# One pair of states transposed by a DMA instead of TensorE, and the operations up to batch 4's first product in another order

## The chip, the core and the metric

The kernel runs on one core of a Trainium2 chip. A core has TensorE (PE, matrix products into PSUM), VectorE (DVE), ScalarE (ACT), GpSimd (POOL) and SyncE (SP); each runs its own queue of instructions in order, and semaphores tie the queues together. The metric is the device time of one launch in microseconds, as the median of several runs.

## The reference

There are 8 batches, 8 heads, 512 tokens, 32 states and 64 numbers per head. Tokens read from the states and states read from the tokens by softmax attention; both results of a batch, 512 + 32 rows of 512 numbers, go through a layer of three products of which the largest counts, and an output product.

```python
scores = scale * np.matmul(x, state.transpose(0, 1, 3, 2))
a = softmax(scores);   xread = np.matmul(a, state)
a2 = softmax(scale * np.matmul(state, x.transpose(0, 1, 3, 2)));   sread = np.matmul(a2, x)
...
x = concatenate([xread, sread]) as [4352, 512]
h = np.maximum(np.maximum(x @ w1, x @ w2), x @ w3)     # 512 -> 768
return (h @ w_out).astype(np.float32)                  # 768 -> 512
```

## The kernel before

The products are reassociated: a token's reading of the states followed by w1, w2, w3 is the attention weights times G = states x weights, so each batch has its own G.

The work is cut into small operations, and their order is written out by hand in the string `PLAN`. One function per operation issues its instructions; each engine takes its own instructions in the order of the plan. `BANKS` and `PAIRS` say which of the four single PSUM banks and two double ones each result takes, in the order of the plan; `PLACES` gives the slot of each SBUF buffer. A result can be written into a bank only when the copies out of the bank's last use are done.

The names that matter here (b is a batch, k a pair of batches, so states 3 serve batches 6 and 7):

- `stc k`, `stt k`, `stp k`: cast the states, transpose them on TensorE (four transposes into a bank), and copy them in two halves into the block layout `bd`. `std k` does the transposing as a DMA from SyncE's queue into an SBUF buffer `stT`; it is defined in the kernel before, and not used by its plan.
- `lx b`, `lxg b g`: load x, whole or half, from GpSimd's queue. `xtd b`: transpose x by DMA, SyncE's queue. `pad b`: copy x with a column of ones, on GpSimd.
- `sc b`, `ex b`, `sum b`: scores (PE), exponentials (ACT), sums and their reciprocals (DVE). `wt b`: the weights, multiplied on GpSimd. `atd b`: the weights transposed by DMA on SyncE's queue into `aT`.
- `sr b`, `srs b`, `srt b`: the states' own reading (PE), scaled (DVE), transposed by DMA (SyncE).
- `g`, `gr b c0 c1`, `gq b c0 c1`: a slice or a run of columns of G on TensorE; `gr` takes a double bank, `gq` two single ones. `gc`, `grc`, `gqc` copy it out, on the engines that the last letters name.
- `l1 b m`: three chains of two products into three banks. `m0` copies the first on ScalarE, `ma` and `mb` take the maximum with the second and third on VectorE, into `ht`.
- `l2 b j`: six products with the output weights; `l2c` copies the result out; `so` stores, from the queue of its last letter.
- `ones` first waits, on GpSimd, for the output weights to land.

SyncE's queue holds the transposing DMAs in the plan's order, GpSimd's the loads, the pads, the weights and most stores. The lines to follow in the profile: 261 (`stt`), 265 (`std`), 271 (`stp`), 291 (`xtd`), 349 (`wt`), 366 (`atd`), 375 (`pad`), 201 and 206 (`lx`, `lxg`), 427 (`g`, `gr`, `gq`), 466 and 469 (`grc`, `gqc`), 477 (`l1`), 492 (`m0`), 497 (`ma`), 505 (`mb`), 514 (`l2`), 526 (`l2c`), 548 (`so`).

Of the kernel before, what the change touches and what calls it, by code (L numbers as in the profile page):

```python
# [15 lines left out]


PLAN = """
    lst 0 A; lxu 0 0 S; zero; clr 0; clr 1; clr 2; clr 3; warm; lxg 0 1; busy 1; xones 1; ident; busy 1;
    lxg 1 0; busy 1; busy 1; stc 0 D; busy 1; busy 1; busy 1; busy 1; busy 1; lxg 1 1; stt 0; busy 1; busy 1;  # L20
    cxu 0 0 D; xt 0 0; stp 0 A; busy 1; xt 0 1; lw 0 2 1; lw 0 1 0; xtc 0 0 D; sc 0 0; xones 0; lw 0 2 2;
    xtc 0 1 D; busy 1; busy 1; sc 0 1; xt 1 0; ex 0 0; ex 0 1; lw 1 3 0; sum 0 0; sum 0 1; xtc 1 0 A; busy 1;
    busy 1; xt 1 1; sc 1 0; xtc 1 1 D; ex 1 0; busy 1; busy 1; sc 1 1; lw 2 3 2; wt 0 1 D; lw 2 3 1; lw 3 4 0;
    wt 0 0 P; lw 3 6 2; at 0 0; sr 0; ex 1 1; sr 1; g 0 0; sum 1 0; wt 1 0 P; g 1 0; atc 0 0 A; at 0 1; at 1 0;
    gc 0 0 A; atc 0 1 A; g 1 1; sum 1 1; gc 1 0 D; atc 1 0 A; srs 0; srs 1; g 0 1; wt 1 1 P; at 1 1; gc 0 1 A;
    l1 0 0; atc 1 1 D; lst 1 A; m0 0 0; lst 3 A; gc 1 1 A; ma 0 0; lw 3 6 1; lw 4 6 0; lxg 2 1; lxg 2 0; l1 0 1;
    m0 0 1; lwo; mb 0 0; g 0 2; g 1 2; ma 0 1; l1 1 0; lst 2 A; gc 0 2 A; mb 0 1; m0 1 0; ma 1 0; l1 0 2;
    mb 1 0; gc 1 2 A; m0 0 2; ma 0 2; l1 1 1; m0 1 1; g 1 3; stc 1 P; mb 0 2; ma 1 1; g 0 3; mb 1 1; stt 1;
# [15 lines left out]
    ma 3 1; l1 3 2; m0 3 2; mb 3 1; ma 3 2; l1 3 3; m0 3 3; mb 3 2; ma 3 3; l1 3 5; wt 4 - P; m0 3 5; mb 3 3;
    l2 2 2; grc 4 1280 1792 A; grc 4 512 1024 A; ma 3 5; mb 3 5; l2c 2 2 D; l1 3 4; so 2 2 4 P; m0 3 4; ma 3 4;
    lx 6; mb 3 4; atd 4; srt 1; ap 0 A; so 2 0 2 P; pad 5; gr 5 1792 2304; gr 5 0 512; grc 5 1792 2304 AD;
    l2 3 0; l2 3 1; grc 5 0 512 D; l2c 3 0 A; l1 4 0; m0 4 0; sc 5 -; ex 5 -; xtd 6; l2c 3 1 D; l2 3 3; ma 4 0;
    gq 5 1024 1280; gr 5 1280 1792; gr 5 512 1024; mb 4 0; sr 5; gqc 5 1024 1280 A; sum 5 -; srs 5; l2c 3 3 A;
    l1 4 1; m0 4 1; ma 4 1; l1 4 2; m0 4 2; mb 4 1; ma 4 2; l1 4 3; m0 4 3; mb 4 2; ma 4 3; l1 4 5; wt 5 - P;
    m0 4 5; mb 4 3; l2 3 2; grc 5 1280 1792 A; grc 5 512 1024 A; ma 4 5; mb 4 5; l2c 3 2 D; l1 4 4; so 3 2 4 P;  # L50
    m0 4 4; ma 4 4; lx 7; mb 4 4; atd 5; srt 2; ap 1 A; so 3 0 2 P; pad 6; gr 6 1792 2304; gr 6 0 512;
    grc 6 1792 2304 AD; l2 4 0; l2 4 1; grc 6 0 512 D; l2c 4 0 A; l1 5 0; m0 5 0; sc 6 -; ex 6 -; xtd 7;
    l2c 4 1 D; l2 4 3; ma 5 0; gq 6 1024 1280; gr 6 1280 1792; gr 6 512 1024; mb 5 0; sr 6; gqc 6 1024 1280 A;
    sum 6 -; srs 6; l2c 4 3 A; l1 5 1; m0 5 1; ma 5 1; l1 5 2; m0 5 2; mb 5 1; ma 5 2; l1 5 3; m0 5 3; mb 5 2;
    ma 5 3; l1 5 5; wt 6 - P; m0 5 5; mb 5 3; l2 4 2; grc 6 1280 1792 A; grc 6 512 1024 A; ma 5 5; mb 5 5;
    l2c 4 2 D; l1 5 4; so 4 2 4 P; m0 5 4; ma 5 4; mb 5 4; atd 6; srt 3; ap 2 A; so 4 0 2 P; pad 7;
    gr 7 1792 2304; gr 7 0 512; grc 7 1792 2304 AD; l2 5 0; l2 5 1; grc 7 0 512 D; l2c 5 0 A; l1 6 0; m0 6 0;
    sc 7 -; ex 7 -; l2c 5 1 D; l2 5 3; ma 6 0; gq 7 1024 1280; gr 7 1280 1792; gr 7 512 1024; mb 6 0; sr 7;
    gqc 7 1024 1280 A; sum 7 -; srs 7; l2c 5 3 A; l1 6 1; m0 6 1; ma 6 1; l1 6 2; m0 6 2; mb 6 1; ma 6 2;
    l1 6 3; m0 6 3; mb 6 2; srt 4; ma 6 3; l1 6 5; wt 7 - P; m0 6 5; mb 6 3; l2 5 2; grc 7 1280 1792 A;  # L60
    grc 7 512 1024 A; ma 6 5; mb 6 5; l2c 5 2 D; l1 6 4; so 5 2 4 P; m0 6 4; ma 6 4; mb 6 4; atd 7; ap 3 A;
    ap 4 A; so 5 0 2 P; srt 6; l1 7 0; srt 7; m0 7 0; l2 6 0; ap 7 D; srt 5; ma 7 0; mb 7 0; l1 7 2; m0 7 2;
    ap 6 A; l2c 6 0 D; ma 7 2; l1 7 3; m0 7 3; ap 5 A; mb 7 2; ma 7 3; l1 7 4; m0 7 4; l2 6 1; l2c 6 1 A;
    ma 7 4; mb 7 4; l1s 0; m0 s 0; l2 6 2; l2c 6 2 A; look; ma s 0; mb s 0; so 6 2 3 S; mb 7 3; l1 7 1; m0 7 1;
    ma 7 1; l1s 2; m0 s 2; mb 7 1; ma s 2; l1 7 5; m0 7 5; mb s 2; ma 7 5; l1s 1; m0 s 1; ma s 1; so 6 0 1 S;
    mb 7 5; l1s 5; m0 s 5; l2p 7 2 384 512; ma s 5; mb s 1; mb s 5; l1s 3; m0 s 3; l2pc 7 2 384 512 A;
    l2p 7 0 384 512; l2p 7 3 256 512; sop 7 2 384 512 P; ma s 3; l2p 7 2 128 384; mb s 3; l2p 7 0 0 128;
    l2pc 7 0 0 128 A; l2pc 7 3 256 512 D; l2p 7 1 0 128; l2pc 7 0 384 512 D; l2p 7 3 0 256; flag;
    l2pc 7 1 0 128 A; l2pc 7 2 128 384 A; l1s 4; m0 s 4; l2 6 3; sop 7 0 0 128 P; ma s 4; sop 7 0 384 512 P;
    mb s 4; l2p s 0 256 512; so 6 1 2 P; l2 s 1; sop 7 3 256 512 A; l2c 6 3 D; l2p 7 2 0 128; sop 7 1 0 128 S;  # L70
    so 6 3 4 A; l2pc 7 3 0 256 D; l2p s 0 0 256; l2pc s 0 256 512 D; sop s 0 256 512 A; l2pc 7 2 0 128 A;
    l2p 7 1 128 384; sop 7 2 0 128 A; l2p 7 0 256 384; l2pc s 0 0 256 A; l2pc 7 1 128 384 A; l2c s 1 D;
    l2p 7 1 384 512; l2p 7 0 128 256; sop 7 3 0 256 S; sop 7 2 128 384 P; l2pc 7 0 256 384 D; sop 7 1 128 384 A;
# [12 lines left out]
PLACES = """
    xT 0:0 1:1 2:2 3:0 4:1 5:2 6:0 7:1;
    e 0:0 1:1 2:0 3:1 4:0 5:1 6:0 7:1;
    a 0:0 1:1 2:0 3:1 4:0 5:1 6:0 7:1;
    aT 0:0 1:1 2:2 3:0 4:1 5:2 6:0 7:1;  # L90
    G 0:0 1:1 2:2 3:0 4:1 5:2 6:0 7:1;
    ht 0:0 1:1 2:2 3:3 4:0 5:1 6:2 7:3;
    osb x00:0 0:1 1:2 2:0 3:1 4:2 5:0 6:1 7:2 s:0;
    xp 2:0 3:1 4:0 5:1 6:0 7:1;
    t0 00:0 01:1 10:2 02:0 11:1 12:2 03:0 13:1 05:2 14:0 04:1 15:2 20:0 21:1 22:2 23:0 25:1 24:2 30:0 31:1 32:2 33:0
        35:1 34:2 40:0 41:1 42:2 43:0 45:1 44:2 50:0 51:1 52:2 53:0 55:1 54:2 60:0 61:1 62:2 63:0 65:1 64:2 70:0
        72:1 73:2 74:0 s0:1 71:2 s2:0 75:1 s1:2 s5:0 s3:1 s4:2;
    t1 00:0 01:1 10:2 02:0 11:1 12:2 03:0 13:1 05:2 14:0 04:1 15:2 20:0 21:1 22:2 23:0 25:1 24:2 30:0 31:1 32:2 33:0
        35:1 34:2 40:0 41:1 42:2 43:0 45:1 44:2 50:0 51:1 52:2 53:0 55:1 54:2 60:0 61:1 62:2 63:0 65:1 64:2 70:0
        72:1 73:2 74:0 s0:1 71:2 s2:0 75:1 s1:2 s5:0 s3:1 s4:2;  # L100
    st 0:0 1:1 2:0 3:1
"""


# [639 lines left out]
```

## Time and profile before

| what | value |
|---|---|
| median of 3 runs | 152.14 us (152.1 to 152.29) |
| span of the profiled execution | 150.5 us; no other time is recorded for it |
| TensorE | 145.1 us busy, 96% of the span |
| VectorE | 118.0 us, 78% |
| ScalarE | 83.2 us, 55% |
| GpSimd | 56.1 us, 37% |

The span reaches from the first to the last instruction, and the runs' time takes in what lies around it. A row of the chain gives start, length, engine, output tile and line; a row of the timeline or of a group gives the output and input tiles, their shapes, the count of instructions, and in brackets the idle time before them with what ended it. Durations of products are those of one instruction, which overlaps with the next; the cost of a product in a full stream is read from the distance of two starts.

### The profile page before, as it was taken

What the parts mean: (1) busy time and instruction counts of PE and PEld (TensorE: products, weight loads), DVE (VectorE), ACT (ScalarE), POOL (GpSimd) and SP (SyncE); (2) the same over time, 40 slices, a digit from 0 to 9 for tenths busy, and PEclk for the clock granted to TensorE, in tenths of its full rate; (3) what the DMA queues carried; (4) which work ended last, traced back from release to release, by engine and by line L of the source; (5) the groups of instructions that cost most, each with busy time, mean ns of one, the idle gap of its engine ahead of it and who ended that gap; (6) DMA issues with size and microseconds to landing.
All of it is one profiled execution on the core that took longest, in us unless ns stands there. A gap on an engine that the chain in (4) does not pass through costs nothing.

```text
span 150.5 us, 3618 instructions
## 1 busy us (share of the span) xinstructions
PE 145.1 (96%) x1422; PEld 72.8 (48%) x1422; DVE 118.0 (78%) x202; ACT 83.2 (55%) x144; POOL 56.1 (37%) x78
## 2 busy tenths in 40 slices
...
GB/s 121 195 188 189 206 230 198 196 97 139 124 97 171 235 182 189 108 209 178 145 102 216 183 139 90 231 183 131 157 4 78 121 175 7 139 0 17 190 199 167
DMA packets 39108, 22.29 MB, mean 148 GB/s; under 512 B 23072, under 2 KB 36896, under 8 KB 39088
## 3 DMA queue, kind: packets, MB, share of 16 engines
...
q8 instruction: 12, 0.20, 0.6%
...
## 4 chain that ended last, share of the span: by engine, by line
PE 88%; DMA 5%; POOL 3%; issue 1%; DVE 1%; ACT 1%; POOLq 0%
PE pw L477 47%; PE po L514 25%; PE pg L427 6%; DMA w<-in_moe_w_dram 5%; PE po L532 4%; PE ps L305 2%; PE psr L391 2%; POOL w L217 1%; POOL x L206 1%; PE pgh L427 1%; ACT G L444 1%; PE pt L261 1%; DVE held L593 0%; PE idle L591 0%; PE pat L358 0%
## 5 line engine op out<-in xcount | busy, mean ns | idle before, releaser
L477 PE MATMUL pw<-aT,G 128*128 128x512 bf16 x288 | 66.7, 379 | 0.0
L492 ACT CAST t<-pw 128x512 bf16<-128x512 f32 (+1 forms) x54 | 30.5, 564 | 27.3 <-PE pw L477 26.4
L497 DVE TENSOR_TENSOR t<-t,pw 128x512 bf16<-128x512 bf16 (+1 forms) x54 | 35.3, 654 | 11.1 <-ACT t L492 8.9
L477 PEld LDWEIGHTS <-G 128*128 128x128 bf16 x288 | 27.1, 98 | 32.8 <-issue 2.1
L514 PE MATMUL po<-wout,ht 128*128 128x512 bf16 x168 | 39.7, 379 | 0.0
L505 DVE TENSOR_TENSOR ht<-t,pw 128x512 bf16<-128x512 bf16 x48 | 32.9, 686 | 4.5
L349 POOL TENSOR_TENSOR a<-e,rden 128x1024 bf16<-128x1024 bf16 (+1 forms) x9 | 14.6, 1622 | 27.2 <-ACT osb L526 11.1
L514 PEld LDWEIGHTS <-ht 128*128 128x128 bf16 x168 | 15.4, 98 | 19.0 <-issue 1.7
L548 POOL DMA_DIRECT2D out_dram<-osb x13 | 7.4, 571 | 27.5 <-ACT t L492 27.5
L466 ACT CAST G<-pg 128x1024 bf16<-128x1024 f32 (+1 forms) x17 | 14.7, 895 | 2.1 <-PE pg L427 2.1
L526 ACT COPY osb<-po 128x512 f32<-128x512 f32 x15 | 8.9, 592 | 9.1 <-PE po L514 9.1
L526 DVE COPY osb<-po 128x512 f32<-128x512 f32 x14 | 9.6, 688 | 3.9 <-PE po L514 3.8
L375 POOL COPY xp<-x 128x1024 bf16<-128x1024 bf16 x12 | 12.3, 1059 | 0.0
L313 ACT ACTIVATE e<-ps 128x1024 bf16<-128x1024 f32 (+1 forms) x10 | 8.5, 854 | 6.7 <-PE ps L305 6.7
L466 DVE CAST G<-pg 128x1024 bf16<-128x1024 f32 (+1 forms) x12 | 11.6, 995 | 0.0
L342 DVE TENSOR_REDUCE seen<-e 128x32 f32<-128x1024 bf16 (+1 forms) x10 | 10.0, 997 | 1.7 <-ACT e L313 1.7
L427 PE MATMUL pg<-w,bd 64*32 64x512 bf16 (+1 forms) x288 | 10.7, 362 | 0.4 <-DMA w<-in_moe_w_dram 0.2
L444 ACT CAST G<-pg 128x768 bf16<-128x768 f32 x10 | 8.0, 810 | 2.7 <-PE pg L427 2.5
...
L249 PE MATMUL idle<-zero 128*128 128x512 bf16 x18 | 7.4, 506 | 1.8 <-DVE zero L225 1.3
L477 PE MATMUL pw<-atp,w 128*128 128x256 bf16 x72 | 8.7, 272 | 0.0
...
## 6 DMA issues: line engine op xcount, KB each, us to landing
out_dram<-osb POOLq DMA_DIRECT2D x12, 512.0 KB, 3.7
x<-in_x_dram POOLq DMA_DIRECT2D x4, 512.0 KB, 7.2
...
```

The lines of the kernel that those rows point to most:

```text
L342: nc.vector.reduce_sum(out=den, in_=parity(e[b], g), axis=AX.X)
L349: times[c](out=parity(a[b], g).rearrange("p j g s n -> p j (g s) n"), in0=parity(e[b], g).rearrange("p j g s n -> p j (g s) n"), in1=rdens ...
L375: nc.gpsimd.tensor_copy(out=xp[b][:, :, :, g * (D + 1):g * (D + 1) + D], in_=v[:, g])
L427: nc.tensor.matmul(p(s, g), bd(b, 2 * s + g)[64 * g:64 * g + 64, g, :], f(w_sb[64 * g:64 * g + 64, s]), start=True, stop=True, tile_positi ...
L444: copier[c[g]](out=G[b][:, g:h, :, m * 128:m * 128 + 128], in_=p[:, g:h, 0:384].rearrange("p g (i f) -> p g i f", i=3))
L466: copier[c[g]](out=v[:, g:h], in_=p[:, g:h, 0:c1 - c0])
L477: nc.tensor.matmul(pw[i][:, 0:n], lhs(i, k), rhs(k), start=(k == 0), stop=(k == nk - 1))
L492: nc.scalar.copy(out=t0s[b, m][:, 0:n], in_=open_ps["l", b, m][0][:, 0:n])
L497: nc.vector.tensor_max(t1s[b, m][:, 0:n], t0s.pop((b, m))[:, 0:n], open_ps["l", b, m][1][:, 0:n])
L505: nc.vector.tensor_max(ht[b][:, m, :], t1s.pop((b, m))[:, 0:n], open_ps.pop(("l", b, m))[2][:, 0:n])
L514: nc.tensor.matmul(p, ht[b][:, m, tokens(b, j)], wout_sb[:, m, :], start=(m == 0), stop=(m == NM - 1))
L526: copier[c[i]](out=o[:, j, i * w:i * w + w], in_=p[:, i * w:i * w + w])
```

## The change

`stt 3` (four transposes on TensorE) becomes `std 3` (one transposing DMA on SyncE's queue, behind `xtd 5` and ahead of `atd 4`), and its copies, `stp 3`, go from ScalarE, ahead of `l2c 0 2`, to GpSimd, behind `pad 5`. Three copies change engines: `l2c 1 0` from VectorE to ScalarE, the first half of `grc 3 0 512` from ScalarE to VectorE, `l2c 2 0` from ScalarE to VectorE. On GpSimd, `pad 2` comes ahead of `ones` and of the loads of batch 3, `lx 4` ahead of the first two stores, which trade places, and `pad 4` ahead of `lx 5`. On SyncE, `srt 0` comes directly behind `atd 2`. On TensorE, `gr 3 1280 1792` comes ahead of `gq 3`. On VectorE, `mb 1 4` comes ahead of its half of `stp 2` and of `stc 3`; on ScalarE, `l2c 2 3` comes ahead of `gqc 4`. Some other operations stand elsewhere in the plan with their place in each queue unchanged. `BANKS` loses the bank of `stt 3` and is renumbered in places, `PAIRS` changes in the third group, and `PLACES` gets `stT 2:0 3:0`. Everything ahead of `gr 2 0 512` and everything from `gr 5 1792 2304` on is in the same order as before.

Cut to the reordered lines, without the two ends that only wrap differently:

```diff
-    ma 1 3; l1 0 5; stc 2 P; g 1 5; gr 2 0 512; mb 1 3; m0 0 5; ma 0 5; l1 1 4; gc 1 5 A; gr 2 1280 1792;
-    m0 1 4; grc 2 0 512 D; mb 0 5; gr 2 512 1024; ma 1 4; grc 2 1280 1792 AD; l1 0 4; m0 0 4; ma 0 4; stt 2;
-    mb 0 4; sc 2 -; ex 2 -; grc 2 512 1024 D; stp 2 AD; stc 3 D; mb 1 4; l2 0 3; l2 0 0; l2c 0 3 A; l2c 0 0 A;
-    sum 2 -; l2 0 1; ones; pad 2; lxg 3 0; lxg 3 1; wt 2 - P; stt 3; xtd 3; l2c 0 1 A; l1 1 5; pad 3;
-    so 0 0 2 P; lx 4; m0 1 5; l2 0 2; ma 1 5; mb 1 5; stp 3 A; l2c 0 2 A; l2 1 0; gq 2 1024 1280; gr 3 0 512;
-    gr 3 1792 2304; l2c 1 0 D; grc 3 1792 2304 D; gqc 2 1024 1280 A; grc 3 0 512 A; atd 2; sr 2; l2 1 1; srs 2;
-    sc 3 -; l1 2 0; m0 2 0; ex 3 -; l2c 1 1 D; l2 1 3; ma 2 0; gq 3 1024 1280; so 0 2 4 P; gqc 3 1024 1280 A;
-    l2c 1 3 A; gr 3 512 1024; gr 3 1280 1792; mb 2 0; sum 3 -; wt 3 - P; atd 3; xtd 4; srt 0; sr 3; srs 3;
...
-    ma 2 4; lx 5; mb 2 4; so 1 0 2 P; pad 4; gr 4 1792 2304; gr 4 0 512; grc 4 1792 2304 AD; l2 2 0; l2 2 1;
-    grc 4 0 512 D; l2c 2 0 A; l1 3 0; m0 3 0; sc 4 -; ex 4 -; xtd 5; l2c 2 1 D; l2 2 3; ma 3 0; gq 4 1024 1280;
-    gr 4 1280 1792; gr 4 512 1024; mb 3 0; sr 4; gqc 4 1024 1280 A; sum 4 -; srs 4; l2c 2 3 A; l1 3 1; m0 3 1;
...
+    gr 2 1792 2304; mb 0 3; l1 1 3; m0 1 3; grc 2 1792 2304 A; xtd 2; ma 1 3; l1 0 5; stc 2 P; g 1 5; m0 0 5; gr
+    2 0 512; l1 1 4; mb 1 3; ma 0 5; gc 1 5 A; m0 1 4; grc 2 0 512 D; mb 0 5; gr 2 1280 1792; gr 2 512 1024; ma
+    1 4; grc 2 1280 1792 AD; l1 0 4; m0 0 4; ma 0 4; stt 2; sc 2 -; mb 0 4; ex 2 -; grc 2 512 1024 D; pad 2; mb
+    1 4; l2 0 3; stp 2 AD; stc 3 D; l2 0 0; l2c 0 3 A; l2c 0 0 A; ones; sum 2 -; lxg 3 0; lxg 3 1; wt 2 - P; xtd
+    3; l2 0 1; l2c 0 1 A; pad 3; l1 1 5; lx 4; m0 1 5; l2 0 2; ma 1 5; l2c 0 2 A; mb 1 5; l2 1 0; gq 2 1024
+    1280; gr 3 0 512; gr 3 1792 2304; so 0 2 4 P; gqc 2 1024 1280 A; l2c 1 0 A; grc 3 0 512 DA; sr 2; grc 3 1792
+    2304 D; l2 1 1; srs 2; atd 2; sc 3 -; srt 0; l1 2 0; m0 2 0; ex 3 -; l2c 1 1 D; so 0 0 2 P; l2 1 3; ma 2 0;
+    gr 3 1280 1792; gq 3 1024 1280; gqc 3 1024 1280 A; mb 2 0; gr 3 512 1024; sum 3 -; l2c 1 3 A; wt 3 - P; atd
+    3; sr 3; l1 2 1; srs 3; m0 2 1; ma 2 1; l1 2 2; m0 2 2; mb 2 1; ma 2 2; l1 2 3; m0 2 3; mb 2 2; ma 2 3; l1 2
...
+    ma 2 4; so 1 2 4 P; gr 4 1792 2304; mb 2 4; xtd 4; pad 4; grc 4 1792 2304 AD; gr 4 0 512; grc 4 0 512 D; l2
+    2 0; l2 2 1; lx 5; l2c 2 0 D; so 1 0 2 P; l1 3 0; m0 3 0; sc 4 -; ex 4 -; xtd 5; std 3; l2c 2 1 D; l2 2 3;
+    gq 4 1024 1280; ma 3 0; l2c 2 3 A; gr 4 1280 1792; gr 4 512 1024; mb 3 0; sr 4; gqc 4 1024 1280 A; sum 4 -;
...
+    4 P; m0 3 4; ma 3 4; lx 6; mb 3 4; atd 4; srt 1; ap 0 A; so 2 0 2 P; pad 5; stp 3 P; gr 5 1792 2304; gr 5 0
...
-    st 0:0 1:1 2:0 3:1
+    st 0:0 1:1 2:0 3:1;
+    stT 2:0 3:0
```

The function that the plan now calls for states 3:

```python
def states_turn_dma(k):
    p = open_ps["st", k] = buffer([128, 4, 128], BF16, "stT", k)
    nc.sync.dma_start_transpose(out=p, in_=st[k].rearrange("p t c d -> p (t c d)"))
```

More of the change, by code (lines that the diff above doesn't have):

```diff
@@ L18 @@
 PLAN = """
[L19 to L28, printed above, removed]
@@ L29 @@
-    gc 1 3 A; l1 1 2; gc 0 3 A; m0 1 2; stp 1 DA; ma 1 2; g 0 4; g 0 5; l1 0 3; gc 0 5 D; g 1 4; mb 1 2;
-    gc 0 4 A; m0 0 3; gc 1 4 A; ma 0 3; gr 2 1792 2304; mb 0 3; l1 1 3; m0 1 3; grc 2 1792 2304 A; xtd 2;
-    ma 1 3; l1 0 5; stc 2 P; g 1 5; gr 2 0 512; mb 1 3; m0 0 5; ma 0 5; l1 1 4; gc 1 5 A; gr 2 1280 1792;
-    m0 1 4; grc 2 0 512 D; mb 0 5; gr 2 512 1024; ma 1 4; grc 2 1280 1792 AD; l1 0 4; m0 0 4; ma 0 4; stt 2;
-    mb 0 4; sc 2 -; ex 2 -; grc 2 512 1024 D; stp 2 AD; stc 3 D; mb 1 4; l2 0 3; l2 0 0; l2c 0 3 A; l2c 0 0 A;
@@ L39 @@
-    l1 2 1; m0 2 1; ma 2 1; l1 2 2; m0 2 2; mb 2 1; ma 2 2; l1 2 3; m0 2 3; mb 2 2; ma 2 3; l1 2 5; m0 2 5;
-    mb 2 3; l2 1 2; grc 3 1280 1792 A; grc 3 512 1024 A; ma 2 5; mb 2 5; l2c 1 2 D; l1 2 4; so 1 2 4 P; m0 2 4;
-    ma 2 4; lx 5; mb 2 4; so 1 0 2 P; pad 4; gr 4 1792 2304; gr 4 0 512; grc 4 1792 2304 AD; l2 2 0; l2 2 1;
-    grc 4 0 512 D; l2c 2 0 A; l1 3 0; m0 3 0; sc 4 -; ex 4 -; xtd 5; l2c 2 1 D; l2 2 3; ma 3 0; gq 4 1024 1280;
-    gr 4 1280 1792; gr 4 512 1024; mb 3 0; sr 4; gqc 4 1024 1280 A; sum 4 -; srs 4; l2c 2 3 A; l1 3 1; m0 3 1;
@@ L44 @@
[L44 to L73, printed above, removed]
@@ L74 @@
-    l2pc 7 1 384 512 D; sop 7 1 384 512 A; l2pc 7 0 128 256 D; sop 7 0 128 256 A; sos 1 S; sop s 0 0 256 S;
-    sop 7 0 256 384 S; hold; vl;
+    lst 0 A; lxu 0 0 S; zero; clr 0; clr 1; clr 2; clr 3; warm; lxg 0 1; busy 1; xones 1; ident; busy 1; lxg 1
+    0; busy 1; busy 1; stc 0 D; busy 1; busy 1; busy 1; busy 1; busy 1; lxg 1 1; stt 0; busy 1; busy 1; cxu 0 0
+    D; xt 0 0; stp 0 A; busy 1; xt 0 1; lw 0 2 1; lw 0 1 0; xtc 0 0 D; sc 0 0; xones 0; lw 0 2 2; xtc 0 1 D;
+    busy 1; busy 1; sc 0 1; xt 1 0; ex 0 0; ex 0 1; lw 1 3 0; sum 0 0; sum 0 1; xtc 1 0 A; busy 1; busy 1; xt 1
@@ new lines @@
+    1; sc 1 0; xtc 1 1 D; ex 1 0; busy 1; busy 1; sc 1 1; lw 2 3 2; wt 0 1 D; lw 2 3 1; lw 3 4 0; wt 0 0 P; lw 3
+    6 2; at 0 0; sr 0; ex 1 1; sr 1; g 0 0; sum 1 0; wt 1 0 P; g 1 0; atc 0 0 A; at 0 1; at 1 0; gc 0 0 A; atc 0
+    1 A; g 1 1; sum 1 1; gc 1 0 D; atc 1 0 A; srs 0; srs 1; g 0 1; wt 1 1 P; at 1 1; gc 0 1 A; l1 0 0; atc 1 1
+    D; lst 1 A; m0 0 0; lst 3 A; gc 1 1 A; ma 0 0; lw 3 6 1; lw 4 6 0; lxg 2 1; lxg 2 0; l1 0 1; m0 0 1; lwo; mb
+    0 0; g 0 2; g 1 2; ma 0 1; l1 1 0; lst 2 A; gc 0 2 A; mb 0 1; m0 1 0; ma 1 0; l1 0 2; mb 1 0; gc 1 2 A; m0 0
@@ new lines @@
+    2; ma 0 2; l1 1 1; m0 1 1; g 1 3; stc 1 P; mb 0 2; ma 1 1; g 0 3; mb 1 1; stt 1; gc 1 3 A; l1 1 2; gc 0 3 A;
+    m0 1 2; stp 1 DA; ma 1 2; g 0 4; g 0 5; l1 0 3; gc 0 5 D; g 1 4; mb 1 2; gc 0 4 A; m0 0 3; gc 1 4 A; ma 0 3;
+    gr 2 1792 2304; mb 0 3; l1 1 3; m0 1 3; grc 2 1792 2304 A; xtd 2; ma 1 3; l1 0 5; stc 2 P; g 1 5; m0 0 5; gr
+    2 0 512; l1 1 4; mb 1 3; ma 0 5; gc 1 5 A; m0 1 4; grc 2 0 512 D; mb 0 5; gr 2 1280 1792; gr 2 512 1024; ma
+    1 4; grc 2 1280 1792 AD; l1 0 4; m0 0 4; ma 0 4; stt 2; sc 2 -; mb 0 4; ex 2 -; grc 2 512 1024 D; pad 2; mb
@@ new lines @@
+    3; sr 3; l1 2 1; srs 3; m0 2 1; ma 2 1; l1 2 2; m0 2 2; mb 2 1; ma 2 2; l1 2 3; m0 2 3; mb 2 2; ma 2 3; l1 2
+    5; m0 2 5; mb 2 3; l2 1 2; grc 3 1280 1792 A; grc 3 512 1024 A; ma 2 5; mb 2 5; l2c 1 2 D; l1 2 4; m0 2 4;
+    ma 2 4; so 1 2 4 P; gr 4 1792 2304; mb 2 4; xtd 4; pad 4; grc 4 1792 2304 AD; gr 4 0 512; grc 4 0 512 D; l2
+    2 0; l2 2 1; lx 5; l2c 2 0 D; so 1 0 2 P; l1 3 0; m0 3 0; sc 4 -; ex 4 -; xtd 5; std 3; l2c 2 1 D; l2 2 3;
+    gq 4 1024 1280; ma 3 0; l2c 2 3 A; gr 4 1280 1792; gr 4 512 1024; mb 3 0; sr 4; gqc 4 1024 1280 A; sum 4 -;
@@ new lines @@
+    srs 4; l1 3 1; m0 3 1; ma 3 1; l1 3 2; m0 3 2; mb 3 1; ma 3 2; l1 3 3; m0 3 3; mb 3 2; ma 3 3; l1 3 5; wt 4
+    - P; m0 3 5; mb 3 3; l2 2 2; grc 4 1280 1792 A; grc 4 512 1024 A; ma 3 5; mb 3 5; l2c 2 2 D; l1 3 4; so 2 2
+    4 P; m0 3 4; ma 3 4; lx 6; mb 3 4; atd 4; srt 1; ap 0 A; so 2 0 2 P; pad 5; stp 3 P; gr 5 1792 2304; gr 5 0
+    512; grc 5 1792 2304 AD; l2 3 0; l2 3 1; grc 5 0 512 D; l2c 3 0 A; l1 4 0; m0 4 0; sc 5 -; ex 5 -; xtd 6;
+    l2c 3 1 D; l2 3 3; ma 4 0; gq 5 1024 1280; gr 5 1280 1792; gr 5 512 1024; mb 4 0; sr 5; gqc 5 1024 1280 A;
@@ new lines @@
+    sum 5 -; srs 5; l2c 3 3 A; l1 4 1; m0 4 1; ma 4 1; l1 4 2; m0 4 2; mb 4 1; ma 4 2; l1 4 3; m0 4 3; mb 4 2;
+    ma 4 3; l1 4 5; wt 5 - P; m0 4 5; mb 4 3; l2 3 2; grc 5 1280 1792 A; grc 5 512 1024 A; ma 4 5; mb 4 5; l2c 3
+    2 D; l1 4 4; so 3 2 4 P; m0 4 4; ma 4 4; lx 7; mb 4 4; atd 5; srt 2; ap 1 A; so 3 0 2 P; pad 6; gr 6 1792
+    2304; gr 6 0 512; grc 6 1792 2304 AD; l2 4 0; l2 4 1; grc 6 0 512 D; l2c 4 0 A; l1 5 0; m0 5 0; sc 6 -; ex 6
+    -; xtd 7; l2c 4 1 D; l2 4 3; ma 5 0; gq 6 1024 1280; gr 6 1280 1792; gr 6 512 1024; mb 5 0; sr 6; gqc 6 1024
@@ new lines @@
+    1280 A; sum 6 -; srs 6; l2c 4 3 A; l1 5 1; m0 5 1; ma 5 1; l1 5 2; m0 5 2; mb 5 1; ma 5 2; l1 5 3; m0 5 3;
+    mb 5 2; ma 5 3; l1 5 5; wt 6 - P; m0 5 5; mb 5 3; l2 4 2; grc 6 1280 1792 A; grc 6 512 1024 A; ma 5 5; mb 5
+    5; l2c 4 2 D; l1 5 4; so 4 2 4 P; m0 5 4; ma 5 4; mb 5 4; atd 6; srt 3; ap 2 A; so 4 0 2 P; pad 7; gr 7 1792
+    2304; gr 7 0 512; grc 7 1792 2304 AD; l2 5 0; l2 5 1; grc 7 0 512 D; l2c 5 0 A; l1 6 0; m0 6 0; sc 7 -; ex 7
+    -; l2c 5 1 D; l2 5 3; ma 6 0; gq 7 1024 1280; gr 7 1280 1792; gr 7 512 1024; mb 6 0; sr 7; gqc 7 1024 1280
@@ new lines @@
+    A; sum 7 -; srs 7; l2c 5 3 A; l1 6 1; m0 6 1; ma 6 1; l1 6 2; m0 6 2; mb 6 1; ma 6 2; l1 6 3; m0 6 3; mb 6
+    2; srt 4; ma 6 3; l1 6 5; wt 7 - P; m0 6 5; mb 6 3; l2 5 2; grc 7 1280 1792 A; grc 7 512 1024 A; ma 6 5; mb
+    6 5; l2c 5 2 D; l1 6 4; so 5 2 4 P; m0 6 4; ma 6 4; mb 6 4; atd 7; ap 3 A; ap 4 A; so 5 0 2 P; srt 6; l1 7
+    0; srt 7; m0 7 0; l2 6 0; ap 7 D; srt 5; ma 7 0; mb 7 0; l1 7 2; m0 7 2; ap 6 A; l2c 6 0 D; ma 7 2; l1 7 3;
+    m0 7 3; ap 5 A; mb 7 2; ma 7 3; l1 7 4; m0 7 4; l2 6 1; l2c 6 1 A; ma 7 4; mb 7 4; l1s 0; m0 s 0; l2 6 2;
@@ new lines @@
+    l2c 6 2 A; look; ma s 0; mb s 0; so 6 2 3 S; mb 7 3; l1 7 1; m0 7 1; ma 7 1; l1s 2; m0 s 2; mb 7 1; ma s 2;
+    l1 7 5; m0 7 5; mb s 2; ma 7 5; l1s 1; m0 s 1; ma s 1; so 6 0 1 S; mb 7 5; l1s 5; m0 s 5; l2p 7 2 384 512;
+    ma s 5; mb s 1; mb s 5; l1s 3; m0 s 3; l2pc 7 2 384 512 A; l2p 7 0 384 512; l2p 7 3 256 512; sop 7 2 384 512
+    P; ma s 3; l2p 7 2 128 384; mb s 3; l2p 7 0 0 128; l2pc 7 0 0 128 A; l2pc 7 3 256 512 D; l2p 7 1 0 128; l2pc
+    7 0 384 512 D; l2p 7 3 0 256; flag; l2pc 7 1 0 128 A; l2pc 7 2 128 384 A; l1s 4; m0 s 4; l2 6 3; sop 7 0 0
@@ new lines @@
+    128 P; ma s 4; sop 7 0 384 512 P; mb s 4; l2p s 0 256 512; so 6 1 2 P; l2 s 1; sop 7 3 256 512 A; l2c 6 3 D;
+    l2p 7 2 0 128; sop 7 1 0 128 S; so 6 3 4 A; l2pc 7 3 0 256 D; l2p s 0 0 256; l2pc s 0 256 512 D; sop s 0 256
+    512 A; l2pc 7 2 0 128 A; l2p 7 1 128 384; sop 7 2 0 128 A; l2p 7 0 256 384; l2pc s 0 0 256 A; l2pc 7 1 128
+    384 A; l2c s 1 D; l2p 7 1 384 512; l2p 7 0 128 256; sop 7 3 0 256 S; sop 7 2 128 384 P; l2pc 7 0 256 384 D;
+    sop 7 1 128 384 A; l2pc 7 1 384 512 D; sop 7 1 384 512 A; l2pc 7 0 128 256 D; sop 7 0 128 256 A; sos 1 S;
```

18 lines of the change are left out of this document (8 added, 10 removed), and 3 rows, old and new, of the table BANKS.

## The prediction

> **What bounds the kernel now.** I read the page first (busy times, chain by line), then the chain in order of time, then the timeline of the stretch that the change reorders, and last the transfers.
>
> ```profile
> span 150.5 us, 3618 instructions
> PE 145.1 (96%) x1422; PEld 72.8 (48%) x1422; DVE 118.0 (78%) x202; ACT 83.2 (55%) x144; POOL 56.1 (37%) x78
> PE 88%; DMA 5%; POOL 3%; issue 1%; DVE 1%; ACT 1%; POOLq 0%
> ```
>
> TensorE is busy for 145.1 of 150.5 us and is 88% of the chain. The reordered part begins at the product `l1 0 5` (about 28.7 us) and ends before batch 4's first product at 75.5 us; nothing before or behind it changes its order. So the question is what TensorE pays for there. The chain in order of time answers it:
>
> ```profile
> 34.75 3.89 PE po L514 x18
> 38.64 0.22 PE pt L261 x4
> 38.86 1.29 PE pw L477 x6
> ...
> 43.80 1.40 PE po L514 x6
> ...
> 64.54 5.30 PE pw L477 x24
> ...
> 79.79 5.30 PE pw L477 x24
> ```
>
> Eighteen products in 3.89 and six in 1.29 are both 0.216 us a product, one behind the other. A group behind a run of small products pays 0.1 more (1.40 against 1.29), in the regular part too (5.30 for 24, where 24 x 0.216 is 5.18). From 64.54 to 79.79 a batch takes 15.25 us, and all of that is TensorE. I see no stall left between 28 and 80 us: time goes down here only by work taken off TensorE, and up by anything that makes TensorE wait.
>
> **The change, part by part.** *The transfer in place of `stt 3`.* This removes four TensorE transposes:
>
> ```profile
> L261 PE MATMUL pt<-ident,st x16: 219/219/314, 5.1 to 38.6; 128*128 128x128 bf16 x16
> 38.48 0.39 PE L261 MATMUL pt<-ident,st 128*128 128x128 bf16 x4
> 38.70 1.46 PE L477 MATMUL pw<-aT,G 128*128 128x512 bf16 x6
> ```
>
> One lasts 219 ns, but they overlap: the four begin at 38.48 and the next product at 38.70, so they cost 0.22 us (0.055 each), which is also the chain's piece. Full durations would be 4 x 0.219 = 0.88, the upper bound; zero is the lower. I take 0.22, because the product behind them shows it. The Trainium skill ("TensorE: Matmul & The Clock Gate", Part 4: PE-mode transpose) gives about 275 ns for one such transpose inside a kernel. An estimate by that page is 4 x 0.275 = 1.1 us saved and 151.04 us; the rows here disagree with it as a price in a full stream.
>
> *Its copies, `stp 3`, leave ScalarE, and `l2c 1 0` and half of `grc 3 0 512` change engines.* The rows around the gap:
>
> ```profile
> 38.68 0.59 ACT L526 COPY osb<-po 128x512 f32<-128x512 f32 x1 [0.71 <-PE po L514]
> 39.33 0.59 ACT L492 CAST t<-pw 128x512 bf16<-128x512 f32 x1
> 39.53 0.35 DVE L344 RECIPROCAL rden<-seen 128x32 f32<-128x32 f32 x1
> 39.81 1.17 ACT L271 COPY bd<-pt 64x512 bf16<-64x512 bf16 x2
> 39.95 0.69 DVE L497 TENSOR_TENSOR t<-t,pw 128x512 bf16<-128x512 bf16 x1
> 39.99 2.75 PE L514 MATMUL po<-wout,ht 128*128 128x512 bf16 x12
> ```
>
> ScalarE loses 1.17 us and gains 0.59 (`l2c 1 0`), and its `grc` shrinks by about 0.4; it has waits to spare there. VectorE's sum stays where it is. But the 0.22 us of transposes also gave ScalarE time. `l2 0 2` takes the PSUM bank that `m0 1 5` empties. `l1 1 5` would now start at 38.48 and `m0 1 5` at 39.11; `l2c 0 1`, unmoved, ends at 38.68 + 0.59 = 39.27, and copies with nothing between them follow up to 0.1 before that end (39.33 to 39.81 is 0.48 for a 0.59 copy). So `m0 1 5` runs from 39.17 or 39.27 to 39.76 or 39.86, and `l2 0 2`, due at 39.99 - 0.22 = 39.77, starts 0 to 0.1 late. I take 0.02, by the follow-on rows, and keep 0.1 for the range.
>
> *VectorE puts `mb 1 4` ahead of its half of `stp 2` and of `stc 3`.* These two come 0.69 us later (a maximum's row, 39.95). Batch 4's runs wait for the one and `std 3` for the other, both after 49.23. Cost zero.
>
> *Runs of batch 3: `gr 3 1280` ahead of `gq 3`.* The same three runs, so the sum on TensorE is the same, but `gqc 3` can start later:
>
> ```profile
> 48.18 0.30 PE L427 MATMUL pgh<-w,bd 64*32 64x256 bf16 x8
> 48.30 0.61 PE L427 MATMUL pg<-w,bd 64*32 64x512 bf16 x16
> 48.55 0.65 ACT L469 CAST G<-pgh 128x256 bf16<-128x256 f32 x2 [0.91 <-PE pgh L427]
> 49.23 5.37 PE L477 MATMUL pw<-aT,G 128*128 128x512 bf16 x24
> ```
>
> One wide run holds the next back by some 0.2 us (the piece of two lasts 0.61, a product 0.38). `gqc 3` moves from 48.55 to 48.55 - 0.22 + 0.2 = 48.53; its first half frees a bank after 0.38, at 48.9, and the next product is due at 49.01. It is covered, by 0.1.
>
> *Batch 2's copies on the way to batch 3.* `l2c 2 0` goes to VectorE, and `l2c 2 3` before `gqc 4`:
>
> ```profile
> 58.98 1.22 DVE L466 CAST G<-pg 128x1024 bf16<-128x1024 f32 x1
> 60.28 1.46 PE L477 MATMUL pw<-aT,G 128*128 128x512 bf16 x6
> 62.04 1.46 PE L514 MATMUL po<-wout,ht 128*128 128x512 bf16 x6
> 63.80 0.65 ACT L469 CAST G<-pgh 128x256 bf16<-128x256 f32 x2 [0.47 <-PE pgh L427]
> 64.47 1.90 PE L477 MATMUL pw<-aT,G 128*128 128x512 bf16 x8
> ```
>
> VectorE would copy `l2c 2 0` from 58.98 + 1.22 - 0.22 = 59.98 to 60.67; the bank goes to the third chain of `l1 3 0`, due at 60.28 + 0.86 - 0.22 = 60.92. Covered by 0.25. `l2 2 3` now ends at 62.04 + 1.46 - 0.22 = 63.28, ScalarE copies it until 63.88, the first half of `gqc 4` follows until 64.2, and `l1 3 1` wants the bank at 64.25: covered by 0 to 0.05, or late by as much. I take zero.
>
> *GpSimd's order.* `pad 2` moves ahead of the wait for the output weights, and the loads of batch 3 behind it start 2 us earlier:
>
> ```profile
> 30.45 2.05 POOL L375 COPY xp<-x 128x1024 bf16<-128x1024 bf16 x2
> 40.04 1.91 POOL L349 TENSOR_TENSOR a<-e,rden 128x1024 bf16<-128x1024 bf16 x1 [6.10 <-ACT t L492]
> 57.94 0.91 POOL L201 DMA_DIRECT2D x<-in_x_dram  x1
> 80.35 1.91 POOL L349 TENSOR_TENSOR a<-e,rden 128x1024 bf16<-128x1024 bf16 x1 [3.69 <-ACT osb L526]
> ```
>
> GpSimd idled 6.10 us before batch 2's weights (`wt 2`), so the gain only lengthens that idle; the weights wait for VectorE's reciprocal (39.53 + 0.35), which does not move. `wt 2` and its turning (`atd 2`) gain nothing. `stp 3` on GpSimd goes into the 3.69 us before `wt 5`: two copies of 64x512, at most 1.06 each by the pad's rows (2.05 for two), so 2.1 us, still covered. The first two stores trade places behind `lx 4`; their buffer is written again only two batches on. What I watch is `pad 4` ahead of the load of batch 5's x (`lx 5`): a pad lasts 2.05 and its clearing, so that load moves from 57.94 to 57.94 + 2.1 - 0.22 = 59.8.
>
> *SyncE's queue.* It runs `xtd 5`, `std 3`, `atd 4`, `srt 1`; `atd 4` feeds `l1 4 0`. `srt 0` moves ahead of `atd 3` into idle time.
>
> ```profile
> 65.24 3.47 SPq L291 DMA_TRANSPOSE xT<-x  x1
> 68.80 1.26 SPq L366 DMA_TRANSPOSE aT<-a  x1
> x<-in_x_dram POOLq DMA_DIRECT2D x1, 512.0 KB, 7.2
> x<-in_x_dram POOLq DMA_DIRECT2D x1, 512.0 KB, 7.9
> DMA to landing us min/median/max: 2.7/2.9/3.2
> 75.52 1.46 PE L477 MATMUL pw<-aT,G 128*128 128x512 bf16 x6
> ```
>
> (The loads are batch 5's and batch 4's; the row of landings is that of `aT`.) With 7.2 us the x lands at 67.0. Then SyncE needs 3.47 for `xtd 5`, 1.26 for `std 3` (no row; less data than `aT`, so its 1.26 as a cap, zero as floor) and 0.1 between each: `atd 4` at 71.9, landed 2.9 later at 74.8. `l1 4 0` is due at 75.30. Covered, by 0.5: the thinnest cover that is not refilled every batch. Everything slow (7.9, 3.47, 1.26, 3.2) gives 75.8, a stall of 0.5. On the other side the load may be faster, since it no longer starts right behind a store: everything fast is a margin over 2 us. I take zero.
>
> **Sum.** -0.22 for the transposes, +0.02 for `l2 0 2`, the rest zero: -0.20 us. The profiled span of 150.5 becomes 150.3. No separate time is given for the profiled execution; the median run is 152.14, which is 1.6 above the span, and I leave that unchanged: 152.14 - 0.20 = 151.94 us. That is 0.13%, less than the 0.2% (0.30 us) that a measurement of this kernel can tell from no change.
>
> **Rivals.** *A: `atd 4` comes late.* Mechanism: `pad 4` before `lx 5` and `std 3` before `atd 4` in two queues in order. It decides from an arrival after 75.52, where the saved 0.22 is gone, and is slower by over 0.3 from 75.82. At 0.5 to 0.8 us of stall the time is 152.4 to 152.7. For it: two queues in order lengthen the same path by 2.1 and 1.3 us. Against: the load begins earlier beside less traffic, and the slow rows must coincide. Chance 0.10.
>
> *B: the gain is eaten by the lockstep.* ScalarE's copy after `l2c 0 1`, and the covers of 0 to 0.1 at `l1 2 1` and `l1 3 1`, each give way by up to 0.1: 152.14 - 0.22 + 0.2 = 152.1. For it: the rows of 39.33 and 63.80 leave almost nothing. Against: in the regular part such covers hold batch after batch at 15.25 us. Chance 0.14.
>
> *C: TensorE also loses a switch.* If the narrow run between the two wide ones, or a product directly behind another without the transposes, spares one of the 0.1 us switches (1.40 against 1.29), the gain is 0.32: 151.8, just faster. For it: such a switch stands in every mixture of kinds. Against: the count of switches stays the same but for the transposes, which showed none. Chance 0.11.
>
> *D: the transposes cost their durations.* 0.88 us of gain by the row's 219 ns, 151.26 us; it needs products that start that much earlier, and 38.48 to 38.70 excludes it nearly. Chance 0.03.
>
> **How the numbers follow.** My forecast has 0.62, A 0.10, B 0.14, C 0.11, D 0.03. Same: forecast and B, 0.76. Faster: C and D, 0.14. Slower: A, 0.10. The range for 8 in 10 reaches from C (151.8, and 0.05 of scatter) to B and the first of A: 151.75 to 152.3.
>
> **What would show it.** In the changed profile: 12 transposes instead of 16, TensorE's products of `l1 1 5` right behind `l2 0 1`, every start after it earlier by 0.2 us, a batch still 15.25 us apart, `wt 2` at 40.0 as before. If I am wrong, look for a gap in TensorE ahead of `l1 4 0`, `l2 0 2`, `l1 2 1` or `l1 3 1`, with SyncE's `aT` transfer, or ScalarE, as what ends it.

## The result and the profile after

| | before | after |
|---|---|---|
| median of 6 runs each | 152.21 us (152.1 to 152.4) | 154.67 us (154.09 to 155.21) |
| ratio of the times, 95% interval | | 1.0155 (1.0125 to 1.0186) |
| span of the profiled execution | 150.5 us | 152.9 us (its time: 154.74) |

The kernel became slower by 2.5 us; the prediction had 151.94, in a range of 151.75 to 152.3. Of the predicted saving of 0.20 us, 0.14 is there, and the loss lies behind the last product.

The page of after, busy times and chain by engine:

```profile
span 152.9 us, 3610 instructions
PE 144.7 (95%) x1418; PEld 72.2 (47%) x1418; DVE 118.4 (77%) x203; ACT 81.5 (53%) x142; POOL 58.2 (38%) x80
PE 87%; DMA 5%; POOL 3%; issue 1%; DVE 1%; POOLq 0%
```

TensorE has four operations fewer (the transposes) and is busy for 0.4 us less. VectorE has one instruction more, 203 against 202. The chain of after in order of time (start, length, engine, tile, line); lines of code stand 3 further on than before:

```profile
34.48 3.88 PE po L517 x18
38.36 1.29 PE pw L480 x6
39.66 2.62 PE po L517 x12
...
48.83 5.36 PE pw L480 x24
...
64.13 5.30 PE pw L480 x24
...
79.38 5.31 PE pw L480 x24
```

The transposes are gone from between 34.48 and 39.66, and from 64.13 to 79.38 a batch takes the same 15.25 us. The start of the program scatters (the first product of the layer begins at 15.18 to 15.94 us in the kernels here that have at most two instructions more), so both kernels are best measured from their first product of the layer (`pw<-aT`) to the last copy on VectorE (`held`). The timelines of before and after at these places (start, length, engine, line, operation, tiles, in brackets the wait before):

```profile
15.72 2.75 PE L477 MATMUL pw<-aT,G 128*128 128x512 bf16 x12
147.74 0.69 DVE L593 CAST held<-idle 128x512 bf16<-128x512 f32 x1 [0.47 <-PE idle L591]
```

```profile
15.45 2.75 PE L480 MATMUL pw<-aT,G 128*128 128x512 bf16 x12
147.33 0.69 DVE L596 CAST held<-idle 128x512 bf16<-128x512 f32 x1 [0.47 <-PE idle L594]
```

Before takes 147.74 - 15.72 = 132.02 us, after 147.33 - 15.45 = 131.88: 0.14 saved. The granted clock of TensorE is 1.00 in both from 15 to 145 us, so it makes no difference there. Yet from `held` to the end of the span before takes 150.5 - 147.7 = 2.7 us and after 152.9 - 147.3 = 5.6. Behind `held` each engine loads a flag and branches over a block that is skipped when the flag is zero (`tc.If(bad != 0, label="again")`, line 674 before, 677 after). The instructions of that line on VectorE and ScalarE, before and then after (queue, instruction, count, nanoseconds of one, first and last start in us):

```profile
L674 DVEq COMPARE_BRANCH  x1: 84/84/84, 148.4 to 148.4; - x1
L674 ACTq COMPARE_BRANCH  x1: 76/76/76, 148.4 to 148.4; - x1
L674 ACTq EVENT_SEMAPHORE  x1: 17/17/17, 148.9 to 148.9; - x1
L674 DVEq EVENT_SEMAPHORE  x1: 21/21/21, 148.9 to 148.9; - x1
```

```profile
L677 ACTq COMPARE_BRANCH  x1: 76/76/76, 148.0 to 148.0; - x1
L677 DVEq COMPARE_BRANCH  x1: 84/84/84, 148.3 to 148.3; - x1
L677 ACTq EVENT_SEMAPHORE  x1: 17/17/17, 148.5 to 148.5; - x1
L677 DVEq EVENT_SEMAPHORE  x1: 21/21/21, 151.8 to 151.8; - x1
```

An `EVENT_SEMAPHORE` is the first instruction behind the branch. VectorE's waits for VectorE's own counter alone, which in after was last raised at 148.04, by `held`, so no other engine holds it back. ScalarE goes on 0.5 us behind its branch in both kernels. VectorE goes on 0.56 us (148.37 to 148.93 in the trace) behind it before, 3.49 us (148.34 to 151.83) after; its branch also comes 0.99 us behind the load of the flag instead of 0.62. All engines meet behind it, and SyncE's wait there for VectorE's counter, the longest of its semaphore instructions, grows from 0.21 to 3.66 us (before, then after):

```profile
L739 SPq EVENT_SEMAPHORE  x14: 17/28/213, 148.0 to 150.4; - x14
```

```profile
L742 SPq EVENT_SEMAPHORE  x14: 17/28/3663, 147.6 to 152.9; - x14
```

The span adds up: the first product is earlier by 0.27, the products save 0.14, and from `held` to the end 2.89 is lost (5.61 us in the trace against 2.72): 2.48, where 152.94 - 150.46 is measured.

### The profile page after: what moved, and what is told of

It reads as the page before. It is cut to its first block, busy times and chain, and to the rows that moved or that the text cites. A ratio compares the mean times of both kernels' runs of the same rounds, so it can differ in the third digit from the quotient of the medians.

```text
span 152.9 us, 3610 instructions
## 1 busy us (share of the span) xinstructions
PE 144.7 (95%) x1418; PEld 72.2 (47%) x1418; DVE 118.4 (77%) x203; ACT 81.5 (53%) x142; POOL 58.2 (38%) x80
## 4 chain that ended last, share of the span: by engine, by line
PE 87%; DMA 5%; POOL 3%; issue 1%; DVE 1%; POOLq 0%
PE pw L480 47%; PE po L517 25%; PE pg L430 6%; DMA w<-in_moe_w_dram 5%; PE po L535 4%; PE ps L308 2%; PE psr L394 1%; POOL w L220 1%; POOL x L209 1%; PE pgh L430 1%; DVE held L596 0%; PE pt L264 0%; PE idle L594 0%; PE pat L361 0%; POOL x L239 0%
## 5 line engine op out<-in xcount | busy, mean ns | idle before, releaser
L469 ACT CAST G<-pg 128x1024 bf16<-128x1024 f32 (+1 forms) x17 | 14.2, 871 | 2.1 <-PE pg L430 2.1
L469 DVE CAST G<-pg 128x1024 bf16<-128x1024 f32 (+1 forms) x13 | 12.2, 973 | 1.8 <-PE pg L430 1.8
```

What stands on the lines that cost most here:

```text
L469: copier[c[g]](out=v[:, g:h], in_=p[:, g:h, 0:c1 - c0])
```

## The experiments

**First question: what makes the branch slow?** The changed kernel's one extra VectorE instruction is `l2c 2 0` and half of `grc 3 0 512` less `l2c 1 0`. That is 325 in the trace instead of 324 (all of VectorE's instructions, the semaphores and branches too; the page's x203 leaves these out). My theory 1 was that the branch's place in the queue matters; rivals were the work itself and the order.

*`e1_one_less_dve`*: the changed kernel, with that copy whole on ScalarE.

```diff
-grc 3 0 512 DA
+grc 3 0 512 A
```

> The changed kernel with grc 3 0 512 copied whole by ScalarE again, which takes one instruction out of VectorE's queue ahead of its last branch (324 in the trace in place of 325). Theory 1 (the number of VectorE's instructions ahead of the branch decides whether what follows the branch is at hand; 3.49 us from branch to the next instruction in the changed kernel, 0.56 before): the wait falls back to about 0.6 us, and the time to 152.0 us (152.21 before, less the 0.14 us that the products show), 151.8 to 152.3. Theory 2 (the order or the transfer itself disturbs the end, whatever the count): it stays at 154.1 to 155.2 us.

*`e2_before_plus_one`*: the kernel before, with one `nc.vector.memset` of a spare 128x1 tile at the start (the lines for the spare tile and the table of operations are not shown).

```diff
+    def extra(n):
+        for _ in range(n):
+            nc.vector.memset(spare, 0.0)
-clr 3; warm;
+clr 3; extra 1; warm;
```

> The kernel before with one more VectorE instruction, a clearing of 128 numbers of a spare tile near the start, where VectorE waits for the states anyway; its order is otherwise as before. Theory 1: the wait behind VectorE's last branch grows from 0.56 to about 3.5 us and the time to 154 to 155 us, though nothing in the middle changes. Theory 2: 152.1 to 152.4 us, as before.

The branch's line in e1, then in e2:

```profile
L677 DVEq COMPARE_BRANCH  x1: 84/84/84, 148.5 to 148.5; - x1
L677 DVEq EVENT_SEMAPHORE  x1: 21/21/21, 149.1 to 149.1; - x1
```

```profile
L679 DVEq COMPARE_BRANCH  x1: 84/84/84, 148.8 to 148.8; - x1
L679 DVEq EVENT_SEMAPHORE  x1: 21/21/21, 152.0 to 152.0; - x1
```

e1 has the whole change but one VectorE instruction less, and its time is 152.24 us, 1.0006 of before beside it (0.9983 to 1.0029): the loss is gone. e2 has nothing of the change but the one instruction, and its time is 155.14, 1.0189 (1.0155 to 1.0224), while its products take 132.02 as before. So the work and the order are not the cause, and one small instruction of 59 ns, put 145 us ahead of the branch, costs some 2.9 us.

**Second question: more instructions, or one place?** *`e4_after_plus_one`* is the changed kernel with `extra 1`, *`e5_before_plus_two`* the kernel before with `extra 2`; both have 326.

> The changed kernel with one more VectorE instruction near the start (326 in the trace). Theory 1 has two forms. If the count has only passed a boundary, everything beyond stays slow: 154 to 155.2 us. If only the one count of 325 is bad, because the branch then stands last in a block, it is fast again: about 152.0 us. Theory 2: 154 to 155.2 us.

> The kernel before with two more VectorE instructions near the start (326 in the trace, the last branch at place 320 counted from 0). Theory 1a (only the count that puts the branch at place 319, last in a block, is bad): 0.6 us behind the branch and 152.1 us, though the kernel with one less took 155.14. Theory 1b (a boundary has been passed, all beyond is slow): 3.3 us behind the branch, 155 us. The rival (order or transfer to blame) has fallen with the second experiment.

The branch's line in e5:

```profile
L679 DVEq COMPARE_BRANCH  x1: 84/84/84, 147.9 to 147.9; - x1
L679 DVEq EVENT_SEMAPHORE  x1: 21/21/21, 148.5 to 148.5; - x1
```

Two more are harmless where one more is not: e5 takes 152.00, 0.9991 of before (0.9973 to 1.001). e4's branch is fast too, 0.61 us, but its time of 153.17, 1.0061 (1.0038 to 1.0084), missed the expected one: from the first product to `held` it takes 133.33 us, where after takes 131.88, because TensorE waited twice, for 0.33 us on a load of weights and for longer here:

```profile
46.61 1.46 PE L485 MATMUL pw<-aT,G 128*128 128x512 bf16 x6 [0.89 <-DMA aT<-a]
```

Batch 2's weights landed 4.5 us behind their issue there, against 2.7 in after. A shift of VectorE by one memset at the start cannot be read as the cause of that; it stays open.

*`e7_before_plus_129`* and *`e8_before_plus_128`* (`extra 129`, `extra 128`) ask whether the place recurs. The memsets delay the start (170.09 and 168.33 us, one run each), so only the branch is compared.

> The kernel before with 129 more VectorE instructions near the start; they delay all that follows by some 8 us, so the time says nothing, and only the wait behind VectorE's last branch is read. Theory 1a with blocks of 128 instructions (VectorE's instruction transfers come at places 64, 192 and 320 of the trace): the branch stands at 318 + 129 = 447, last in a block again, and the wait is 3 to 3.5 us. If blocks do not matter: 0.6 us.

> The same with 128 more: the branch at place 446, one ahead of the last place. Theory 1a: 0.6 us behind the branch. A theory in which long queues are slow at the branch: 3 us, as with 129.

The branch's line in e7, then in e8:

```profile
L679 DVEq COMPARE_BRANCH  x1: 84/84/84, 164.0 to 164.0; - x1
L679 DVEq EVENT_SEMAPHORE  x1: 21/21/21, 167.2 to 167.2; - x1
```

```profile
L679 DVEq COMPARE_BRANCH  x1: 84/84/84, 164.6 to 164.6; - x1
L679 DVEq EVENT_SEMAPHORE  x1: 21/21/21, 165.2 to 165.2; - x1
```

The place recurs after 128 instructions. Counted in the traces, with VectorE's first instruction as 0:

| branch's place | kernels | from the branch to the next instruction |
|---|---|---|
| 317, 318 | e10; before, e1, e3, e6, e9, e11 | 0.57; 0.56 us |
| 319 | after, e2 | 3.49, 3.23 |
| 320 | e4, e5 | 0.61, 0.61 |
| 446 | e8 | 0.57 |
| 447 = 319 + 128 | e7 | 3.23 |

The transfers of instructions point to a reason, without showing it. Instructions come in pieces of 8192 bytes on one queue (q14 in the page), which does not name the engine that they are for. The page counts those within the span, before and then in e8; e2 has the same line as e8:

```profile
q14 instruction: 8, 0.07, 0.2%
```

```profile
q14 instruction: 9, 0.07, 0.2%
```

Counted in the traces from the first instruction to the last transfer, also behind the span, there are 9 pieces in every kernel with the branch at 317 or 318, 10 with 319, 320 and 446, and 11 with 447. That fits pieces of 128 VectorE instructions, of 64 bytes each, with a new piece behind place 319. In e4 and e5, whose branch would be the first of the new piece, the additional transfer comes at 144.91 and 143.2, some 4.7 us ahead of the branch. In after and e2, whose branch would be the last of the old piece, there is no such early transfer. There two transfers come while VectorE stands; the later one starts at 149.31 and 149.53, 0.7 to 1.0 us behind the branch, lasts under 0.5 us, and VectorE goes on only 2.5 us after its start. The Trainium skill ("Runtime: NRT & Kernel Launch", Instruction fetch mechanics) says that an engine reads ahead in sequence only, and that a taken branch to a target outside the fetched window waits for a transfer. A wait of 3.2 to 3.5 us behind a taken branch fits that; that the same branch waits only 0.6 us at the places beside it does not follow from it, and the page's blocks of 256 instructions do not agree with the 128 here. That the stall is a fetch is argued from the transfers; what the runs show is that the number of VectorE's instructions ahead of the branch decides. Why 319 is bad and 318 is not stays open. Each queue also has a `BRANCH_PREFETCH_HINT` near its start (at 0.8 us on VectorE), and no run tests what it does for this branch.

**Third question: is the rest of the prediction right?** *`e3_transfer_only`* is the kernel before with states 3 turned by the transfer, and nothing else; *`e9_transfer_only_again`* repeats it in 5 rounds (only the operations that change are shown; one bank fewer and a place for `stT` go with them).

```diff
-stt 3;
-stp 3 A;
-xtd 5;
+xtd 5; std 3;
-pad 5;
+pad 5; stp 3 P;
```

> The kernel before with the states of pair 3 turned by the transfer alone (std 3 behind xtd 5, its copies on GpSimd behind pad 5), everything else in the old order. VectorE's queue has as many instructions as before. Theory 1: no wait at the end, the four transposes are saved: 152.0 us, 151.8 to 152.2. Theory 2, in the form that the transfer is to blame: 154 us or more. In the form that the order is to blame: 152.0 as well.

> The transfer alone, as in the third experiment, in more rounds, as the version that may beat both kernels: the products showed 0.22 us less between the first product and the last copy (131.80 against 132.02), so 0.2 us under the kernel before, ratio 0.9987. If the saving were only an accident of that run, ratio 1.000.

The timeline of e3 where the transposes were, to be compared with 38.48 to 39.99 of before:

```profile
34.06 4.05 PE L513 MATMUL po<-wout,ht 128*128 128x512 bf16 x17
37.94 1.46 PE L476 MATMUL pw<-aT,G 128*128 128x512 bf16 x6
39.26 2.75 PE L513 MATMUL po<-wout,ht 128*128 128x512 bf16 x12
```

From the first product to `held` e3 takes 131.80 and e9 131.82: 0.22 and 0.20 less than before. The times are 151.92 and 152.07, ratios 0.9989 (0.9973 to 1.0005) and 0.9991 (0.9972 to 1.001): as small as expected, and still not to be told from no change.

*`e6_order_only`* is e1 with states 3 turned on TensorE as before (against e1, shown in the same way).

```diff
-l2 0 1;
+l2 0 1; stt 3;
-ma 1 5; l2c 0 2 A;
+ma 1 5; stp 3 A; l2c 0 2 A;
-xtd 5; std 3;
+xtd 5;
-pad 5; stp 3 P;
+pad 5;
```

> The changed kernel with states 3 turned by TensorE again at the old place, their copies on ScalarE, and grc 3 0 512 whole on ScalarE, so that VectorE has 324 instructions: the new order without the transfer. From the distance between the first product and the last VectorE copy (132.02 us before, 131.80 with the transfer alone, 131.96 with both) the order by itself should cost 0.1 to 0.2 us: 152.2 to 152.4 us. If the order were a gain, under 152.0.

It takes 152.23, 1.0007 (0.9993 to 1.002), and 132.16 from product to `held`, 0.14 more than before; 0.12 of this stands at the scores of batch 3, behind the unsplit copy of `grc 3 0 512`. The order alone gains nothing.

*`e10_two_transfers`* turns states 2 by a transfer as well, which e3 leaves on TensorE (against e3, shown in the same way).

```diff
-stc 2 P;
+stc 2 P; std 2;
-ma 0 4; stt 2;
+ma 0 4;
```

> The transfer alone, and states 2 turned by a second transfer (std 2 behind xtd 2) with l2 0 3 in the bank that stt 2 had. If only TensorE's work counts here, another 0.22 us goes: 131.58 from the first product to the last copy. But l2 0 3 would come to its fifth product at 35.23 us on the clock of the kernel before, and VectorE writes the maximum that it reads (mb 0 4) until 35.33: then only 0.08 to 0.1 us goes, 131.7, and VectorE's maximum is what ends a new wait.

The second transfer saved 0.06 us at `l1 1 5`, where 0.08 to 0.1 was expected. The median of its 13 runs is 152.48, from 151.85 to 158.27, and the ratio without the two longest is 1.0032 (1.0004 to 1.0059): no gain. The profiled execution is the longest, 158.27 us, and in it batch 4's weights were late; the wait, and SyncE's transfers:

```profile
PE pw L476 <- DMA aT<-a: 3.5, 1, 3.5
67.54 3.09 SPq L290 DMA_TRANSPOSE xT<-x  x1
70.79 1.19 SPq L264 DMA_TRANSPOSE stT<-st  x1
72.08 1.26 SPq L365 DMA_TRANSPOSE aT<-a  x1
```

That is the wait that the prediction's rival A names, in another kernel and by another cause: `aT` was issued at 72.08, and it landed 6.5 us later, where the prediction's slowest was 3.2. Why is not known, and one execution does not show that the second transfer brings it about.

**Last: the changed kernel without its extra instruction.** *`e11_after_l2c20_on_act`* keeps the split copy and gives `l2c 2 0` back to ScalarE, which leaves 324 instructions on VectorE.

```diff
-l2c 2 0 D
+l2c 2 0 A
```

> The changed kernel with l2c 2 0 on ScalarE as before, and grc 3 0 512 split as in the change: VectorE has 324 instructions again, by another removal than in the first experiment. Place 319 theory: 0.6 us behind the branch, and the change's own gain in full: 131.9 us from the first product to the last copy, 152.0 us. If it was grc 3 0 512 itself that disturbed the end: 154 us or more.

It takes 152.06 us against 152.33 for before beside it, 0.9974 (0.9957 to 0.9991), with the branch at 0.56 us. The interval just leaves out 1, but 0.27 us is less than the 0.30 that the prediction calls the least that can be told from no change, and it is one of several versions, so that it beats before is not settled. Its profiled execution, at 152.35 the longest of its ten runs, shows 132.11 us from first product to `held`, where 131.9 was expected, and no less than before; between those ends it lost 0.22 to waits and bank order around 23.05, where TensorE stood for a load of weights:

```profile
23.05 0.52 PE L430 MATMUL pg<-w,bd 64*32 64x384 bf16 x16 [0.15 <-DMA w<-in_moe_w_dram]
```

Without that it would be 131.89, close to after's value and 0.13 under before; the rest of the 0.27 us the profile does not show.

## Why the prediction was wrong, step by step

- **The step that failed** is "the rest zero", by which "The profiled span of 150.5 becomes 150.3": what lies behind the last product was taken as fixed without a reason, and so one VectorE instruction more was priced at nothing. The moves of copies between engines were priced by their time alone ("VectorE's sum stays where it is"), and even that was off, since half of `grc 3 0 512` comes on top: 118.0 became 118.4 us, and 202 instructions 203. The stretch from `held` to the end measured 5.61 us instead of 2.72, +2.89, and e2, with one instruction more and nothing else, 155.14 against 152.11 for before beside it. I had not looked at the stretch behind `held`. None of the rivals, the slower one among them, had a place behind the last product. The 1.6 us that the sum adds for what lies around the span was not the error: in after's profiled execution it is 154.74 - 152.94 = 1.8.
- **The transposes, -0.22**: right. At `l1 1 5`, measured from the first product, before is at 22.98, after at 22.75, e3 at 22.76. The 0.055 us for each transpose holds, and D falls with it. The Trainium skill's 275 ns ("TensorE: Matmul & The Clock Gate", Part 4: PE-mode transpose) does not hold as a price in a full stream.
- **`l2 0 2` late by 0.02**: right, 0.02 to 0.03 (its chain piece is 2.62 instead of 2.59 for 12).
- **"The rest zero", as far as the last product**: nearly. The 24 products `l1 2 1` to `l1 2 5` take 5.36 us in after, 5.30 before and in e3. 0.06 us is lost ahead of the third chain of `l1 2 5`, which takes the bank that `ma 2 3` empties; this was not in the prediction. So 0.14 is left of the 0.20: a small part of rival B, at another place than B named.
- **`gqc 3`, `l1 3 1`, `l2c 2 0`, `wt 2`, `stp 3` on GpSimd**: no wait of TensorE ahead of any of them. GpSimd's idle time ahead of `wt 2` only grew, as forecast, from 6.10 to 7.54 us. Two copies of `stp 3` took 2.24 us (2.1 was my bound):

```profile
76.19 2.24 POOL L274 COPY bd<-stT 64x512 bf16<-64x512 bf16 x2
```

- **SyncE's queue**: right in kind, the cover larger than said. The load of batch 5's x, the three transfers, the landing of `aT` and batch 4's first product, in after:

```profile
59.51 0.90 POOL L204 DMA_DIRECT2D x<-in_x_dram  x1
66.27 3.07 SPq L294 DMA_TRANSPOSE xT<-x  x1
69.39 1.26 SPq L268 DMA_TRANSPOSE stT<-st  x1
70.76 1.24 SPq L369 DMA_TRANSPOSE aT<-a  x1
aT<-a SPq DMA_TRANSPOSE x1, 2.7
75.28 1.29 PE pw L480 x6
```

`aT` lands at 70.76 + 2.7 = 73.5, and the product is due at 75.28: 1.8 us of cover instead of 0.5. The load of x began 1.57 us later than before, as the working has it (the reason against rival A, that it begins earlier, is wrong), but it landed 6.7 us behind its issue instead of 7.2, and `xtd 5` took 3.07 instead of 3.47. `std 3` cost 1.26 us of the queue, the cap that I had set. In e10 `aT` was too late by 3.5, by its landing of 6.5 us and not by the order of the queues.
- **C, a switch spared**: not seen; the saving in e3 is 0.22 at most.
